# Identity matmuls of TensorE in the opening and the tail, stores moved to POOL, and a planner with other constants

## The chip, the cores and the metric

One core of a Trainium2 chip runs the whole program. The metric is the device time of one execution in microseconds (us). TensorE (PE) multiplies, with weight loads on a track of their own (PEld); VectorE (DVE) and ScalarE (ACT) do elementwise work and empty the accumulator banks; GpSimd (POOL) and SyncE (SP) mostly issue DMAs.

## What is computed

```python
B, S, D = 8, 3136, 256                     # d_qk = 64
scores = (1.0 / S) * np.matmul(z, z.transpose(0, 2, 1))
attn = np.maximum(scores, 0.0) ** 2
x = u * np.matmul(attn, v)

proj = x @ w_proj                          # D -> 3 D
x1, x2, x3 = proj[..., :D], proj[..., D:2 * D], proj[..., 2 * D:]
X2 = np.fft.rfft(x2, n=S, axis=1)
H = np.fft.rfft(filter_fft, n=S, axis=0)[None]
x2_conv = np.fft.irfft(X2 * H, n=S, axis=1)
out = (x1 * x2_conv * x3) @ w_out
```

Inputs and output are float32; the kernel multiplies in bfloat16 and accumulates in float32.

## The kernel before

The sequence of 3136 is written as 64 x 49, so that the Fourier transform splits into a stage over 64 and a stage over 49, both done as matmuls. The sequence is cut into 25 tiles of 128 rows (the last has 64) and, for the query side, into seven chunks of 512, 512, 512, 512, 512, 256 and 320 columns. The work of one batch is:

- Scores, kind "S": zT against itself, 64 rows deep, two or four matmuls side by side in the array, into a pair of banks (`ps_s`). ACT applies the relu (`R_t`, line 1767), DVE or ACT squares (`A_t`, lines 1776 and 1774).
- Weighing, kind "W": v against the squares, accumulated in two banks of their own (`ps_o`). Some squares are used a second time as their mirror images: SP transposes them by DMA into `M_t`, `M2e_t`, `M2o_t` (line 1700). DVE multiplies the sum by u (`xT_t`, line 1818).
- Projection, kind "FA" (for the last batch partly "FZ"): to the gates (`to_gates`: x1 and x3, copied as `x_t` and multiplied on DVE into `gate_t`, line 1160), and to the spectrum (`to_spectrum`: x2, then the first stage of the transform, stored to a scratch in DRAM by line 964).
- Spectrum, kind "Q" (`add_spectrum`): loads of the scratch (line 994), the second stage as quads of 64 x 64 tiles, two multiplications by H on DVE (line 1248), inverse quads, copies into `gs_t` (for the last batch also `M2o_t`, `A_t`, `uT_t`), and stores to a second scratch (`put`, line 1293).
- End, kinds "FB" and "FZ" (`add_end`): loads of the second scratch (line 1006), the last stage of the inverse with T, the product with the gates on DVE (`yT_t`, line 1334), the product with w_out, the copy to `ost_t` (or another free tile) and the store to the output (`store`, line 1394).

No engine's order is written out by hand. The kernel makes tasks with costs, and a planner (`Plan.go`) lays them out: again and again it takes, over all five queues, the task that can start first by its own clock, emits it, and notes when its results and buffers will be there. For PE it chooses among the kinds (`pick_pe`), by the fields of `RULES`: whether weighing work left over (`backlog`, `ample`) is enough to wait for banks, how long it stays with the scores while the next pair is not free (`stay`), when quads go ahead (`first`, `lead`), and when projections and ends may go before weighing (`pace`, `full`). For work that either DVE or ACT can do, `pick` decides, with `give` as the weight of the tasks that would be held up on the second engine. It charges PE 0.096 us whenever it goes between the scores' tile shape and full-array work. A change of a constant, of a cost or of a due time (`late`) therefore can change the order on every engine.

Banks: three pairs for scores and quads; single banks of the same pairs for projections and ends (`one_slots`).

The ends of a batch are interleaved with the next batch's attention. For the last batch but one (b = 6) three chunks are ended so and four are held back, kind "FZ", until the last batch needs something to do while its spectrum goes through DRAM. For the last batch (b = 7) the chunks end in the order `FINAL`, and its outputs go in two halves, one from POOL and one from SP; the last chunk goes from SP alone:

```python
            if split and c == cs[-1]:
                for k, e_ in enumerate(oe):
                    s_ = on("SP", lambda i0=2 * k, n=min(2, nt - 2 * k), store=store: store(i0, n), 0.9, [e_, *behind], prio=1, moves=0.9)
```

The opening: SP loads z of the first batch in three parts, POOL loads v and u with a cast, POOL and DVE make the identity (`ident`) that PE's transposes need, and the DFT tables are made on DVE, ACT and PE beside the first attention.

Of the kernel before, what the change touches and what calls it, by code (L numbers as in the profile page):

```python
# [12 lines left out]
P = 128  # L13
# [15 lines left out]
SPEC_LAG = 1  # L29
LATE_F = 6.0  # L30
LATE_OUT = 2.0
AFTER = (1, 3, 5, 6)
FINAL = (0, 2, 4, 6, 1, 3, 5)
ZP, ZL = 0, 0.0
# [1 line left out]
REACH = 2  # L36
Rule = namedtuple("Rule", "backlog ample stay first lead pace full give")
STEP = 50.0
RULES = [Rule(0.5, 5.0, 0.15, 0, 1, 0.55, 3.5, 0)]
SHARE = {0: 1, 2: 3}  # L40

ISSUED = "issued"
# [14 lines left out]
def c_pe(*ns):  # L57
    return sum(n / 2400 + 0.003 for n in ns)
# [123 lines left out]
class Plan:  # L182
# [151 lines left out]
    def pick(self, e):  # L334
# [18 lines left out]
                best = (key, s, task)  # L353
        return best and (best[1], best[2], e)

    def go(self):
        while True:
            got = []
            x = self.pick_pe()
            if x:  # L360
                got.append((x[0], 0, x[1], "PE", x[2]))
            for i, e in enumerate(self.pend):
                x = self.pick(e)
                if x:
                    got.append((x[0], i + 1, x[1], e, None))
            if not got:
                break
            start, _, task, e, k = min(got, key=lambda g: g[:2])
            if k:
                self.queues[k].remove(task)  # L370
                half = k in ("S", "Q")
                if half != (self.mode == "S") and self.mode:
                    start += 0.096
                    self.quarters, self.quad_run, self.score_run = half and self.soon, 0, 0
                self.score_run += k == "S"
                if k == "Q":
                    self.quad_run += 1
                    if self.score_run and not self.quarters:
                        start += 0.092
                    self.quarters = True  # L380
                self.mode = "S" if half else k
                if k == "W":
                    self.credit = min(self.credit + self.rule(start).pace, 2.0)
                elif k != "S":
                    self.credit = max(self.credit - task.cost["PE"], -2.0)
            self.run(task, e, start)
        left = sum(len(q) for q in self.queues.values()) + sum(len(q) for q in self.pend.values())
        assert not left, f"{left} tasks left over"
# [3 lines left out]
def kernel(  # L392
# [307 lines left out]
    plan.free["POOL"] = 12.0  # L700
    plan.free["SP"] = 3.0
    plan.free["DVE"] = 1.5


    def after(task, at):
# [282 lines left out]
    def load_spec(src, j0, nj, deps, late=0.0, home=l_p):  # L988
        box = {}

        def go():
            box["t"] = home.tile([P, 8, D], BF16)
            for rows, part in by_row(src, box["t"], 2 * j0, 2 * nj):
                nc.sync.dma_start(out=part, in_=rows)

        t = on("SP", go, 1.3, [*deps, *((d, ISSUED) for d in loads[-1:])], [home.slots], moves=0.6 * nj, late=late)
        return in_order(t), box

    def load_c(src, c, deps, home):
        t0, nt = T0[c], len(tiles[c])  # L1000
        box = {}

        def go():
            box["t"] = home.tile([P, 4, D], BF16)
            view = src[ds(t0 * P, nt * P), :].rearrange("(t p) d -> p t d", t=nt)
            nc.sync.dma_start(out=box["t"][:, 0:nt, :], in_=view)

        if home is c_p:
            return in_order(on("SP", go, 0.45, [*deps, *((d, ISSUED) for d in loads[-1:])], [home.slots], moves=0.4 * nt, late=LATE_C)), box
        return on("SP", go, 0.45, deps, [home.slots], moves=0.4 * nt), box  # L1010

    def sides(x):
        return x[:, 0:D], x[:, D : 2 * D]
# [200 lines left out]
    def add_spectrum(b, puts):  # L1214
# [9 lines left out]
        for g in range(NJ // 2):  # L1224
            own = not final or g % 2 == 0
            xh = xh_p if own else R_p
            mine = set_of[g]
            per, gh = 2 * len(mine), outs[sets.index(mine)]
            if g % 2 == 0:
                ldb[0] = load_spec(D1[b % 2], 2 * g, 4, puts, LATE_LOAD * (not final), homes[g // 2] if final else l_p)  # L1230
            ld, ibox = ldb[0]
            xb = {}

            def mm(ps, g=g, xb=xb, ibox=ibox, xh=xh):
                xb["x"] = xh.tile([P, 2, 4, D], BF16)
                forward(ps, slot(ibox["t"], 2 * g % 4), g)

            def ev(e, h, p, xb=xb):
                copy(e, xb["x"][:, 0, ds(2 * h, 2), :].rearrange("p c d -> p (c d)"), p)

            a0, evs = add_quads(mm, ev, c_quads(g), [ld, *deps0], [xh.slots])
            if g % 2:
                a0.frees.append((ld, 0))

            def mul(i, g=g, xb=xb):
                x = xb["x"][:].rearrange("p i (j c) d -> p i j c d", c=2)
                h = H[:, ds(2 * g, 2), i].unsqueeze(2).to_broadcast([P, 2, 2, D])
                nc.vector.tensor_tensor(x[:, 1 - i], x[:, 0], h, ALU.mult)  # L1248

            def add(xb=xb):  # L1250
                x = xb["x"][:].rearrange("p i (j c) d -> p i c j d", c=2)
                nc.vector.tensor_tensor(x[:, 1, 0], x[:, 1, 0], x[:, 0, 1], ALU.subtract)
                nc.vector.tensor_tensor(x[:, 1, 1], x[:, 1, 1], x[:, 0, 0], ALU.add)

            cost = c_dve2(4 * D)
            w_ = on("DVE", lambda mul=mul: mul(0), cost, evs, prio=ZP)
            w_ = on("DVE", lambda mul=mul: mul(1), cost, [w_], prio=ZP, lat=ZL)
            z_ = w_ if final else on("DVE", add, 2 * c_dve2(2 * D), [w_], prio=ZP)

            def inv(g=g, xb=xb, z_=z_, a0=a0, gh=gh, mine=mine, per=per):  # L1260
                new = g == mine[0]
                if new:
                    gb[0] = {"es": [], "firsts": []}
                gx = gb[0]

                def mm(ps, g=g, new=new):
                    if new:
                        gx["g"] = gh.tile([P, 2 * per, D], BF16)
                    z, y = (slot(xb["x"][:, i], 0) for i in range(2))
                    if final:  # L1270
                        inverse2(ps, y, z, g)
                    else:
                        inverse(ps, y, g)

                def ev(e, h, p, g=g):
                    copy(e, gx["g"][:, ds(2 * (2 * (g - mine[0]) + h), 2), :].rearrange("p c d -> p (c d)"), p)

                a, evs = add_quads(
                    mm, ev, c_quads(g, 1 + final), [z_, *gx["firsts"], *(minus_task if final else [])], [gh.slots] if new else []
                )  # L1280
                gx["firsts"] = [a]
                if new:
                    gx["g0"] = a
                a.frees.append((a0, 1))
                inverses.append(a)
                gx["es"] += evs
                if g != mine[-1]:
                    return
                j0 = 2 * mine[0]

                def put():
                    for rows, part in by_row(D2[b % 2], gx["g"], 2 * j0, 2 * per):
                        nc.sync.dma_start(out=rows, in_=part)

                p_ = on("SP", put, 1.2, gx["es"], moves=0.5 * per, late=LATE_D2 * (not final))
                p_.frees.append((gx["g0"], 1))
                lasts.append(p_)

            behind.append(inv)
            if g >= SPEC_LAG:  # L1300
                behind.pop(0)()
# [4 lines left out]
    def add_end(b, lasts, gtasks, cs, kind="FB", src=c_p, dsts=(o_p,), late=0, behind=(), then=(), split=False, mids=(y_p,)):  # L1306
        for at, c in enumerate(cs):
            t0, nt = T0[c], len(tiles[c])
            w = CHUNKS[c]
            dst, mid = dsts[at % len(dsts)], mids[at % len(mids)]  # L1310
            ld, cb = load_c(D2[b % 2], c, lasts, src)
            yb = {}
            ys = []
            firsts = []
# [33 lines left out]
                ys.append(e_)  # L1348
            ob = {}
            oe = []  # L1350
            for i0 in range(0, nt, 2):
                n = min(2, nt - i0)
                last = min(P, w - (i0 + n - 1) * P)
                box = {}

# [38 lines left out]
                        by.dma_start(out=r[:, n2 : n2 + hi - lo, :], in_=ob["o"][ds(j * N1, N1), i0 : i0 + hi - lo, :])  # L1394

            if split and c == cs[-1]:
                for k, e_ in enumerate(oe):
                    s_ = on("SP", lambda i0=2 * k, n=min(2, nt - 2 * k), store=store: store(i0, n), 0.9, [e_, *behind], prio=1, moves=0.9)
            elif split:
                s_ = on("POOL", lambda nt=nt, store=store: store(0, nt, (0,), nc.gpsimd), 0.6, [*oe, *behind], moves=0.22 * nt)  # L1400
                s_ = on("SP", lambda nt=nt, store=store: store(0, nt, (1,)), 0.8, [*oe, *behind], prio=1, moves=0.22 * nt)
            else:
                s_ = on("SP", lambda nt=nt, store=store: store(0, nt), 1.3, [*oe, *behind], prio=1, moves=0.45 * nt, late=LATE_OUT * (dst is o_p))
# [508 lines left out]
```

## Time and profile before

| | us |
|---|---|
| three runs, median (lowest to highest) | 992.51 (992.26 to 992.87) |
| the profiled execution | 993.72 |
| its span, first to last instruction | 991.5 |

Busy time over the span:

| engine | busy us | share | instructions |
|---|---|---|---|
| PE | 958.2 | 97% | 6831 |
| PEld | 472.2 | 48% | 6831 |
| ACT | 867.9 | 88% | 1187 |
| DVE | 819.4 | 83% | 1465 |
| POOL | 191.7 | 19% | 409 |

The chain of work that ended last is 82% PE, 7% DVE, 4% ACT and 2% DMA. Matmuls are pipelined and their ends are modelled, so a busy PE is not a PE at its peak: the distance between two starts says how fast it streams. POOL issues DMAs of the software kind, which took 2.5 to 5.3 us from issue to landing, by size. On the last row of POOL stands a drain of 8.45 us, from 982.3 us on.

By stage, idle time of PE (length less busy time): 7.9 us from 0 to 10, 1.5 us from 10 to 20, 0.6 us from 20 to 30, 1.5 us from 30 to 40, 4.6 us in the 800 us from 100 to 900, 4.0 us from 940 to 960, 1.7 us from 960 to 970, 1.3 us from 970 to 980. After 981.8 us no matmul runs.

### The profile page before, as it was taken

What the parts mean: (1) busy time and instruction counts of PE and PEld (TensorE: products, weight loads), DVE (VectorE), ACT (ScalarE), POOL (GpSimd) and SP (SyncE); (2) the same over time, 40 slices, a digit from 0 to 9 for tenths busy, and PEclk for the clock granted to TensorE, in tenths of its full rate; (3) what the DMA queues carried; (4) which work ended last, traced back from release to release, by engine and by line L of the source; (5) the groups of instructions that cost most, each with busy time, mean ns of one, the idle gap of its engine ahead of it and who ended that gap; (6) DMA issues with size and microseconds to landing.
All of it is one profiled execution on the core that took longest, in us unless ns stands there. A gap on an engine that the chain in (4) does not pass through costs nothing.

```text
span 991.5 us, 19534 instructions
## 1 busy us (share of the span) xinstructions
PE 958.2 (97%) x6831; PEld 472.2 (48%) x6831; DVE 819.4 (83%) x1465; ACT 867.9 (88%) x1187; POOL 191.7 (19%) x409
## 2 busy tenths in 40 slices
PE   6999999999999999999999999999999999999985
PEld 2344544455444554446444454444544455544643
DVE  7876689987899878987789877898779988799774
ACT  6988898988998898899989999889989899999773
POOL 5132311132013210313111220121202231001001
PEclk9999999999999999999999999999999999999978
DMA  9889958979979799978998786998889978984576
GB/s 154 150 171 199 165 118 128 187 137 185 202 174 176 147 194 187 186 156 133 200 197 178 148 152 152 205 191 158 153 196 186 203 138 165 202 213 106 154 229 197
DMA packets 332343, 170.32 MB, mean 172 GB/s; under 512 B 242442, under 2 KB 307786, under 8 KB 332244
## 3 DMA queue, kind: packets, MB, share of 16 engines
q1 hardware_dynamic: 304068, 136.59, 63.4%
q0 software_dynamic: 28176, 32.48, 23.2%
q8 instruction: 54, 0.88, 0.4%
q14 instruction: 45, 0.37, 0.1%
HBM read 90.26 MB, written 53.35 MB: 145 GB/s over the span
## 4 chain that ended last, share of the span: by engine, by line
PE 82%; DVE 7%; ACT 4%; DMA 2%; issue 2%; SPq 1%; POOL 0%; POOLq 0%; DVEq 0%; ACTq 0%
PE ps_o_t L521 48%; PE ps_s L521 34%; DVE A_t L1776 2%; ACT R_t L1767 2%; DVE xT_t L1818 1%; DMA M2e_t<-A_t 1%; DVE xh L1248 1%; DMA ost_t<-in_z_dram 1%; DMA conv_in_t<-spec 1%; DVE gate_t L1160 1%; DVE yT_t L1334 1%; SPq L646 1%; ACT A_t L1774 0%; ACT x_t L554 0%; DMA M_t<-A_t 0%
## 5 line engine op out<-in xcount | busy, mean ns | idle before, releaser
L1767 ACT ACTIVATE R_t<-ps_s 128x1024 f32<-128x1024 f32 (+4 forms) x512 | 466.9, 963 | 57.1 <-PE ps_s L521 55.0
L521 PE MATMUL ps_o_t<-A_t,v_t 128*128 128x512 bf16 (+3 forms) x2084 | 459.5, 354 | 2.9 <-DVE A_t L1776 2.1
L521 PEld LDWEIGHTS <-v_t 128*128 128x128 bf16 (+2 forms) x2878 | 250.6, 98 | 257.8 <-issue 73.2
L1776 DVE TENSOR_TENSOR A_t<-R_t 128x1024 bf16<-128x1024 f32 (+3 forms) x283 | 313.9, 1123 | 64.2 <-ACT R_t L1767 61.1
L1774 ACT ACTIVATE A_t<-R_t 128x1024 bf16<-128x1024 f32 (+3 forms) x213 | 211.7, 1007 | 3.1 <-DMA M2e_t<-A_t 1.7
L521 PE MATMUL ps_s<-zT_t 64*64 64x512 bf16 (+5 forms) x1485 | 170.8, 361 | 2.0 <-ACT R_t L1767 1.0
L604 POOL COPY tick<-xT_t 1x1 bf16<-1x1 bf16 x54 | 13.8, 256 | 681.6 <-DVE xT_t L1818 681.6
L521 PEld LDWEIGHTS <-zT_t 64*64 64x64 bf16 (+1 forms) x1518 | 53.9, 101 | 109.7 <-issue 93.7
L521 PE MATMUL ps_s<-xT_t,wp 128*128 128x512 bf16 (+2 forms) x430 | 103.7, 353 | 2.4 <-DVE gate_t L1160 0.9
L554 ACT ACTIVATE x_t<-ps_s 128x512 bf16<-128x512 f32 (+2 forms) x148 | 81.7, 583 | 19.7 <-PE ps_s L521 12.5
L1818 DVE SCALAR_TENSOR_TENSOR xT_t<-ps_o_t,uT_t 128x256 bf16<-128x256 f32 (+2 forms) x224 | 76.1, 381 | 22.8 <-PE ps_o_t L521 14.4
L1248 DVE TENSOR_TENSOR xh<-xh,H 128x1024 bf16<-128x1024 bf16 x120 | 82.0, 683 | 2.1 <-ACT xh L554 0.9
L521 PE MATMUL ps_o_t<-M_t,v_t 128*128 128x512 bf16 (+2 forms) x352 | 81.8, 353 | 0.0
L1160 DVE TENSOR_TENSOR gate_t<-ps_s,x_t 128x256 bf16<-128x256 f32 (+2 forms) x216 | 71.2, 381 | 6.6 <-PE ps_s L521 4.6
L1334 DVE TENSOR_TENSOR yT_t<-ps_s,gate_t 128x512 bf16<-128x512 f32 (+2 forms) x99 | 57.9, 613 | 10.3 <-PE ps_s L521 10.0
L558 DVE CAST xh<-ps_s 128x512 bf16<-128x512 f32 x71 | 47.3, 685 | 22.8 <-PE ps_s L521 19.5
L521 PEld LDWEIGHTS <-wp 128*128 128x128 bf16 x448 | 42.3, 98 | 49.6 <-issue 15.2
L595 POOL DMA_DIRECT2D un_t<-in_u_dram x112 | 59.8, 554 | 5.6 <-issue 2.7
L614 POOL DMA_DIRECT2D v_t<-in_v_dram x112 | 59.4, 552 | 6.4 <-issue 3.8
L521 PE MATMUL ps_s<-wp,xT_t 128*128 128x256 bf16 x398 | 56.7, 272 | 0.5 <-ACT R_t L1767 0.3
L521 PE MATMUL ps_s<-wo,yT_t 128*128 128x256 bf16 (+1 forms) x344 | 52.0, 273 | 1.6 <-DVE yT_t L1334 1.3
L554 ACT ACTIVATE s_t<-ps_s 128x512 bf16<-128x512 f32 (+1 forms) x79 | 44.9, 592 | 5.5 <-PE ps_s L521 2.1
(154 smaller groups left out, 833.1 us busy)
## 6 DMA issues: line engine op xcount, KB each, us to landing
out_dram<-ost_t SPq DMA_DIRECT2D x66, 256.0 KB
spec<-s_t SPq DMA_DIRECT2D x96, 128.0 KB
spec_in_t<-spec SPq DMA_DIRECT2D x60, 192.0 KB
spec<-gs_t SPq DMA_DIRECT2D x60, 192.0 KB
v_t<-in_v_dram POOLq DMA_DIRECT2D x80, 128.0 KB, 4.5
un_t<-in_u_dram POOLq DMA_DIRECT2D x80, 128.0 KB, 4.9
conv_in_t<-spec SPq DMA_DIRECT2D x33, 256.0 KB
out_dram<-ost_t SPq DMA_DIRECT2D x19, 128.0 KB
```

What stands on the lines that cost most here:

```text
L521: wrote(nc.tensor.matmul(o, *args, **kw), o)
L554: got = nc.scalar.activation(out_, in_, AF.Copy)
L558: got = nc.vector.tensor_copy(out_, in_)
L595: nc.gpsimd.dma_start(out=t[ds(j * N1, N1), lo - t0 : hi - t0, :], in_=x[:, n2 : n2 + hi - lo, :])
L614: nc.gpsimd.dma_start(out=t[ds(j * N1, N1), ds(v_at(a), (b - a) * D)], in_=r[:, n2 + a - lo : n2 + b - lo, :].rearrange("p t d -> p (t d)"),)
L1160: got = nc.vector.tensor_tensor(g[:, ::-1] if h == 0 else g, p, x, ALU.mult)
L1248: nc.vector.tensor_tensor(x[:, 1 - i], x[:, 0], h, ALU.mult)
L1334: got = nc.vector.tensor_tensor(yb["y"][:, dh, 0:w], p, gates[b, c, dh][:, 0:w], ALU.mult)
L1767: has_read(nc.scalar.activation(blocks(box["R"], n, cw)[:rows], p, AF.Relu), p)
L1774: nc.scalar.activation(a, r, AF.Square)
L1776: nc.vector.tensor_tensor(a, r, r, ALU.mult)
L1818: nc.vector.scalar_tensor_tensor(x, f, inv_s2, ut, ALU.mult, ALU.mult)
```

## The change

- Fillers. Before the planner emits a task, `fill` looks whether PE is free long enough before it. In the opening (before 13 us of the plan's time), or when no scores and no weighing are left, it emits a matmul of the identity by the identity, 128 x 512, into a free single bank, as long as it ends 0.25 us before the next task is due. Its result is not read. In the opening a filler is charged double. PE counts as free from 1.8 us on.
- Outputs of b = 6 are stored from POOL instead of SP.
- Spectrum of the last batch: of the three stores of each set, SP issues one or two (two for the last two sets) and POOL the others.
- Last chunk of the last batch: its two tiles are multiplied and copied one by one, and its two halves are stored from SP and from ACT.
- The rule has other constants, and the loads of the spectrum and of some chunks other costs for the planner.

```diff
+LATE_POOL = 1.2
+WARM, SPARE = 13.0, 0.25
-RULES = [Rule(0.5, 5.0, 0.15, 0, 1, 0.55, 3.5, 0)]
+RULES = [Rule(1.25, 5.0, 0.05, 0.5, 1, 0.5, 3.0, 1.0)]
...
+    def fill(self, until):
+        t = self.free["PE"]
+        opening = t < WARM
+        cost = c_pe(512) * (1 + opening)
+        if not opening and (self.queues["S"] or self.queues["W"] or not any(self.queues.values())):
+            return False
+        start = t + 0.096 * (self.mode == "S")
+        if until < start + cost + 0.096 * (self.mode == "S") + SPARE or self.singles.when() > start:
+            return False
+        self.bank, self.got = self.singles, [(self.singles, self.singles.take(start))]
+        self.filler()
+        self.free["PE"] = start + cost
+        self.singles[self.got[0][1]] = start + cost
+        if self.mode:
+            self.mode, self.quarters = "W", False
+        return True
...
             start, _, task, e, k = min(got, key=lambda g: g[:2])
+            if self.fill(start):
+                continue
...
+    plan.free["PE"] = 1.8
+    plan.singles = one_slots
+    plan.filler = lambda: matmul(bank(), ident[:], ident[:].unsqueeze(1).to_broadcast([P, 4, P]), start=True, stop=True)
...
-        t = on("SP", go, 1.3, [*deps, *((d, ISSUED) for d in loads[-1:])], [home.slots], moves=0.6 * nj, late=late)
+        t = on("SP", go, 1.6, [*deps, *((d, ISSUED) for d in loads[-1:])], [home.slots], moves=0.4 * nj, late=late)
...
-        return on("SP", go, 0.45, deps, [home.slots], moves=0.4 * nt), box
+        return on("SP", go, 0.55, deps, [home.slots], moves=0.3 * nt), box
...
-                def put():
-                    for rows, part in by_row(D2[b % 2], gx["g"], 2 * j0, 2 * per):
-                        nc.sync.dma_start(out=rows, in_=part)
-
-                p_ = on("SP", put, 1.2, gx["es"], moves=0.5 * per, late=LATE_D2 * (not final))
+                def put(part=slice(0, 3), by=nc.sync):
+                    for rows, t in by_row(D2[b % 2], gx["g"], 2 * j0, 2 * per)[part]:
+                        by.dma_start(out=rows, in_=t)
+
+                if final:
+                    n = 1 + mine[0] // 2 % 2
+                    p_ = on("SP", lambda: put(slice(0, n)), 0.55 * n, gx["es"], moves=0.25 * per)
+                    lasts.append(
+                        on("POOL", lambda: put(slice(n, 3), nc.gpsimd), 0.55 * (3 - n), gx["es"], moves=0.25 * per, late=LATE_POOL)
+                    )
+                else:
+                    p_ = on("SP", put, 1.2, gx["es"], moves=0.5 * per, late=LATE_D2)
...
+            step = 1 if split and c == cs[-1] else 2
...
-            for i0 in range(0, nt, 2):
-                n = min(2, nt - i0)
+            for i0 in range(0, nt, step):
+                n = min(step, nt - i0)
...
             if split and c == cs[-1]:
-                for k, e_ in enumerate(oe):
-                    s_ = on("SP", lambda i0=2 * k, n=min(2, nt - 2 * k), store=store: store(i0, n), 0.9, [e_, *behind], prio=1, moves=0.9)
+
+                def both_queues(nt=nt, store=store):
+                    store(0, nt, (0,))
+                    store(0, nt, (1,), nc.scalar)
+
+                s_ = on("SP", both_queues, 0.6, [*oe, *behind], prio=1, moves=0.45 * nt)
+            elif b == B - 2:
+                s_ = on(
+                    "POOL", lambda nt=nt, store=store: store(0, nt, by=nc.gpsimd), 1.2, [*oe, *behind],
+                    moves=0.45 * nt, late=LATE_POOL,
+                )
```

## The prediction

> **What bounds the kernel now.** I read the slices of busy time first, then the busy time by stage.
>
> ```profile
> PE   6999999999999999999999999999999999999985
> PEclk9999999999999999999999999999999999999978
> ...
> 0.00:10.00 10.00, 2.12 (x10) 0.76 (x11) 6.73 (x37) 4.88 (x8) 8.32 (x25) 1.00 0.79 147
> 10.00:20.00 10.00, 8.49 (x52) 3.96 (x51) 7.43 (x16) 6.60 (x9) 5.14 (x11) 1.00 1.03 173
> 20.00:30.00 10.00, 9.38 (x50) 3.27 (x49) 9.99 (x10) 7.66 (x8) 0.00 (x0) 1.00 1.22 145
> ...
> 700.00:800.00 100.00, 99.98 (x689) 47.38 (x691) 84.64 (x146) 89.44 (x117) 16.80 (x34) 1.00 0.94 183
> ...
> 940.00:960.00 20.00, 16.05 (x191) 10.32 (x192) 16.75 (x29) 15.55 (x31) 0.00 (x0) 0.78 0.87 247
> 960.00:970.00 10.00, 8.26 (x55) 4.19 (x55) 6.00 (x15) 4.73 (x10) 0.00 (x0) 0.75 0.49 147
> 970.00:980.00 10.00, 8.69 (x95) 6.82 (x94) 8.33 (x18) 5.27 (x11) 2.16 (x4) 1.00 0.79 225
> ```
>
> The columns of a stretch are its length, busy time of PE, PEld, DVE, ACT and POOL, granted clock, DMA share and GB/s. PE is the bound from about 40 to 940 us: the eight stretches of 100 us from 100 to 900 leave 4.6 us of PE idle in all. Only the opening and the tail have room, and only the tail shows a clock below 1. Cut finer, the clock is 1.00 up to 951.3, 0.50 from 951.4 to 965.0 and 1.00 again until 985. In the opening that column has no record before about 12 us, so there I read spacing in the order of time:
>
> ```profile
> 11.40 2.10 PE L521 MATMUL ps_o_t<-A_t,v_t 128*128 128x512 bf16 x6
> ...
> 12.90 1.04 ACT L554 ACTIVATE xT_t<-ost_t 128x448 bf16<-128x448 f32 x2 [2.49 <-DMA ost_t<-in_z_dram]
> ...
> 16.20 1.02 PE L521 MATMUL ps_o_t<-A_t,v_t 128*128 128x512 bf16 x4 [0.30 <-DVE A_t L1776]
> ```
>
> The first six matmuls of 512 columns start 0.42 us apart up to 12.68 us and 0.22 us apart after it, as the four at 16.20 do: PE runs at half speed until about 12.7 us. But what is waited for at 12.9 us is the third load of z.
>
> Last the tail, where I followed the queues beside PE:
>
> ```profile
> 936.59 4.04 SPq L1394 DMA_DIRECT2D out_dram<-ost_t  x4
> 940.72 3.52 SPq L994 DMA_DIRECT2D spec_in_t<-spec  x6
> ...
> 962.43 2.01 SPq L1293 DMA_DIRECT2D spec<-A_t  x3
> 964.54 1.32 SPq L1293 DMA_DIRECT2D spec<-uT_t  x3
> 967.09 4.09 SPq L1006 DMA_DIRECT2D A_t<-spec  x7
> ...
> 962.39 1.89 PE L521 MATMUL ps_o_t<-xT_t,wp 128*128 128x512 bf16 x4
> 964.07 1.49 PE L521 MATMUL ps_s<-xT_t,wp 128*128 128x512 bf16 x4
> ```
>
> The last batch's spectrum loads stand behind four output stores of the batch before; its last spectrum stores stand in one queue, and the loads of its inverse wait for them. The eight gate matmuls at 962.39 take 3.4 us for what eight times 0.216 us would be.
>
> **The change part by part.**
>
> *Fillers.* The built program's order has 38 of them on PE: 12 before and between the first z transposes and scores, 26 from the last batch's spectrum on. At 0.43 us cold the opening's cost 5.2 us, at 0.216 us the tail's cost 5.6 us; both lie in time in which the plan has PE waiting. If the cover is gone, a filler delays what stands behind it by its own length, and in the tail by two changes of tile shape more (about 0.10 us each, below).
>
> Opening: seven fillers begin when the identity is there (1.6 us), so the clock is up somewhere between 5 and 9 us instead of 12.7. What then runs at full speed is the second z transpose (1.06 us), six weighings (2.10 us) and the second scores: about 1.4 us earlier at 13.4 us. The third z load at 12.9 does not move, and the order now gives its two casts that ACT did (0.57 us each) to DVE, ahead of a square of 1.22 us, so most is lost again, and from 20 to 30 us DVE is busy 9.99 of 10. Bounds: 2.2 us gained (half of the 4.4 us that matmuls stream at half speed before 12.7, summed from their starts), 0.9 lost (two late fillers). I take **-0.7**, nearer the third load.
>
> Tail, multiplications by H (947 to 961): DVE works through 16 of 0.60 us and eight copies almost without gaps, and one copy of 0.6 us goes to ACT; a clock at full speed shortens the last quads and the first waits (0.44, 0.38 and 0.16 us on DVE). **-0.9**, bounds -1.5 and 0.
>
> Tail, gates (962 to 970.7): eight matmuls at full clock save 3.4 - 1.7 = 1.7 us, if the loads behind come as early. SP begins the stores of uT_t at 964.54 although the copies ended at 963.2, because A_t's three were still being issued; now SP issues two of each three and POOL the third (0.55 us, in parallel). The last SP issue ends about 1.7 us earlier, but POOL's small DMAs (8 KB of z) landed 2.5 us after issue, so I count 0.9 for the queue and 0.5 for the copies: loads from 965.7, not 967.09. **-1.4**, bounds -1.9 and 0.
>
> *Stores of batch 6 on POOL.* Fourteen issues of 0.54 us, 7.6 us, on a queue that was idle from 916 to 975; behind them now stand POOL's seven spectrum stores, not due before 953. SP's loads at 940.72 can go once the stores of s_t have landed, 2.6 to 3.2 us earlier. But the order also moves 3.3 to 3.5 us of end work of batch 6 and gates (16 matmuls with wo among it) to before the last weighing: from 931.3 to the first spectrum matmul PE had 12.9 us of stream in 15.7 us; now it has 9.6 us in 12.5 us. The wait stays 2.8 us and the gain is used up: **0**, bounds -1.6 (all of the idle) and +1.2 (the landing later than I think).
>
> *Last chunk.* One copy of 0.60 us becomes two of 0.38 us, and its second store goes from SP to ACT. But the last engine to finish is POOL: its last store is issued at 982.33 and its closing drain lasts 8.45 us, while SP has finished at 988.1 and waits until 990.9. The chunk's stores are off that path: 0 from this, **-0.3** for the work in front of it, bounds -0.8 and +0.3.
>
> *New constants of the rule and new costs.* They reorder the 900 us in between. The count of runs of scores and quads that interrupt full-array matmuls goes from 289 to 297; by the starts in the trace the median change of shape costs 0.096 us in and 0.105 to 0.125 us out, so +1.7. Against it 23 squares of 1024 move from ACT to DVE and copies move back: at the means by shape (1.218 us on DVE, 1.078 us on ACT; copies 0.685 and 0.61) DVE gets 8.7 us busier and ACT 9.8 us less busy, of 819 and 868. ACT carries the relus that free the banks for the scores. Bounds: -2.9 (all 4.6 us of idle gone, less 1.7) and +10.4 (all of DVE's 8.7 seen by PE, plus 1.7). I take **0**: the runs' price is paid back by ACT's relief.
>
> Sum: -0.7 - 0.9 - 1.4 + 0 - 0.3 + 0 = **-3.3 us**. The profiled execution took 993.72 us, 2.2 us of it outside the span of 991.5; it becomes 990.4. The median of the runs is 1.2 us below that execution, so I forecast 992.5 - 3.3 = **989.2 us**.
>
> [...]
>
> **The rivals.**
>
> *The clock falls anyway.* From 951.4 to 961.5 PE was called busy 8.5 of 10.1 us, but by quads of a quarter of the array, and the clock came back only after 3.3 us of full-array gates. The fillers are full-array, but between the first spectrum matmul and the gates there are 18, 3.9 us in some 15. If that is too thin, the multiplications keep 0.5 of 0.9 at most and the gates 0.9: -0.7 - 0.5 - 0.9 + 0.3 = -1.8, **990.7 us**. Against it: the clock held until 951.3 through 937 to 947, where PE was far from full.
>
> *ACT was the hidden wait.* If its relief ends all PE idle in the middle (-2.9) and the tail reaches its bounds (another -1.2), **985.1 us**. For it: ACT is at 90% there and the waits for a free bank end on relus; against it, the rows leave only 4.6 us.
>
> *DVE becomes what the weighings wait for.* Place: 50 to 930 us, the matmuls into ps_o_t. A square on DVE takes 0.14 us longer, and DVE gets 8.7 us more work. If half of that shows on PE (4.4) and nothing is paid back for the runs (1.7), the middle costs 6.1: **995.3 us**. It decides once about 3.6 of the 8.7 us surface. Against it: PE waited for squares only 2.1 us in all; for it: PE has no slack of its own, so whatever is late there stays.
>
> **How the numbers follow.** Forecast 0.45, clock 0.16, ACT 0.15, DVE 0.24. Differences within 0.2%, about 2 us, can't be told from none. The forecast and ACT's case are faster: 0.60. The clock's is the same: 0.16. DVE's is slower: 0.24. The range goes from just below ACT's case to DVE's, 984.5 to 995.5; the forecast's own is 987 to 991.
>
> **What would show it.** Matmuls of 512 columns 0.22 us apart from 9 us on, not 13; a granted clock of 1.00 from 940 to 980; SP's loads of spec_in_t directly behind the stores of s_t; spec<-uT_t within 0.3 us of its copies; first matmul T,A_t about 2 us earlier after the last weighing; PE idle of about 4.6 us in the middle stretches. The forecast is wrong if the middle shifts by more than 2 us, which the last weighing's place shows (931 us before, 3.5 us of moved work on top), or if POOL's drain grows with its 21 more stores.

## The result, and the profile after

| | before | after |
|---|---|---|
| runs on the same chip, median (lowest to highest), us | 992.38 (992.05 to 992.87) | 998.47 (996.59 to 999.5) |
| the profiled execution, us | 993.72 | 999.5 |
| its span | 991.5 | 997.7 |

The ratio is 1.0055, 95% interval 1.0042 to 1.0068: slower by 5.5 us, where 3.3 us faster was forecast. The interval is from four runs; the kernel with the same program except for six stores (e12 below) spread from 988.8 to 1000.2 us in eleven runs, so the size is known less well than the interval says.

First the slices of the page, then the stretches, of the changed kernel (columns as before: length, busy time of PE, PEld, DVE, ACT, POOL, granted clock, DMA share, GB/s):

```profile
PE   7998999999999999999999999999989999999985
PEclk9999999999999999999999999999999999999998
```

```profile
0.00:10.00 10.00, 6.18 (x26) 2.01 (x27) 7.35 (x39) 5.29 (x8) 8.47 (x25) 1.00 0.76 146
...
90.00:95.00 5.00, 4.95 (x27) 2.39 (x27) 3.89 (x6) 2.55 (x4) 0.29 (x1) 1.00 1.26 149
95.00:100.00 5.00, 2.30 (x16) 1.03 (x14) 1.01 (x2) 3.78 (x6) 0.00 (x0) 1.00 1.11 153
...
700.00:800.00 100.00, 95.13 (x654) 44.63 (x663) 84.00 (x146) 87.51 (x116) 18.10 (x39) 0.98 0.92 177
...
940.00:960.00 20.00, 16.96 (x169) 10.42 (x167) 15.30 (x32) 13.06 (x27) 6.05 (x12) 1.00 0.72 228
960.00:970.00 10.00, 8.48 (x119) 3.88 (x121) 7.95 (x14) 7.39 (x15) 3.17 (x6) 1.00 0.47 124
```

The fillers do what the change says: the tail, which was at 0.78 and 0.75, is at 1.00 throughout, and the clock is up at 4.4 us. What is new stands in the middle, where PE had almost no idle time before. From 95 to 100 us it is busy 2.30 of 5 us, and from 700 to 800 us it loses 4.9 us and a little of its clock.

The waits of PE from 50 to 930 us (us in all, times, longest) say for what. Changed kernel, then the kernel before:

```profile
PE ps_o_t L542 <- issue: 4.3, 27, 0.2
PE ps_o_t L542 <- DVE xT_t L1859: 2.6, 5, 1.1
PE ps_s L542 <- ACT s_t L575: 2.6, 1, 2.6
PE ps_s L542 <- DMA spec_in_t<-spec: 2.5, 2, 1.9
PE ps_s L542 <- DVE xT_t L1859: 1.5, 7, 0.3
```

```profile
PE ps_o_t L521 <- DVE xT_t L1818: 0.5, 1, 0.5
PE ps_s L521 <- DVE xT_t L1818: 0.4, 2, 0.2
```

The first row is no wait: this trace has 6784 matmuls for 6881 weight loads, and the 27 gaps are places where a matmul's record is missing. The trace of e12 (below), with the same order and 6881 of both, has no such row. Two single waits, of 2.6 us at 95 us and of 1.9 us (with 0.6 behind it) at 738 us, are the largest; the second is followed by a clock of 0.50 from 741.7 to 745.1. The waits for `xT_t`, which DVE makes from the sums of the weighings, grew from 0.9 to 4.1 us.

To place the loss I take the time at which the last weighing is read (the last `xT_t` on DVE):

| us, profiled executions | before | after | difference |
|---|---|---|---|
| last weighing read | 932.0 | 942.1 | +10.1 |
| from there to POOL's closing drain | 50.3 | 44.4 | -5.9 |
| the drain | 8.45 | 10.27 | +1.8 |
| from there to the end of the span | 0.8 | 0.9 | +0.1 |

Of the 10.1 us, 3.5 are matmuls that the new order streams ahead of the last weighing instead of behind it (36 of them, with 8192 columns in all, counted in e12's trace, at 0.216 us for 512 columns, the distance of two starts at full clock in both traces), so the middle lost 6.6 us net and the tail's work gained 2.4. Of the 6.6, 2.0 are 20 more changes of tile shape at 0.1 us; the opening stood 1.6 us earlier, though the trace of before is the latest of ten there (34.1 us where their mean is 33.0); waits and the half clock make up the rest, some 6.2. This sum closes only to a few us: by their rows, the waits from 50 to 930 us grew by 8.0 (from 3.6 to 11.6 us, missing records left out).

### The profile page after: what moved, and what is told of

It is laid out like the page before. It is cut to its first block, busy times and chain, and to the rows that moved or that the text cites. A ratio compares the mean times of both kernels' runs of the same rounds, so it can differ in the third digit from the quotient of the medians.

```text
span 997.7 us, 19593 instructions
## 1 busy us (share of the span) xinstructions
PE 951.8 (95%) x6784; PEld 471.1 (47%) x6881; DVE 831.6 (83%) x1463; ACT 861.3 (86%) x1190; POOL 205.8 (21%) x430
## 5 line engine op out<-in xcount | busy, mean ns | idle before, releaser
L542 PE MATMUL ps_o_t<-A_t,v_t 128*128 128x512 bf16 (+3 forms) x1992 | 446.2, 353 | 11.0 <-issue 4.4
L1817 DVE TENSOR_TENSOR A_t<-R_t 128x1024 bf16<-128x1024 f32 (+3 forms) x306 | 343.3, 1133 | 62.4 <-ACT R_t L1808 61.7
L542 PEld LDWEIGHTS <-v_t 128*128 128x128 bf16 (+1 forms) x2878 | 251.0, 98 | 259.2 <-issue 67.9
L1815 ACT ACTIVATE A_t<-R_t 128x1024 bf16<-128x1024 f32 (+3 forms) x190 | 186.0, 990 | 5.2 <-issue 3.7
L542 PE MATMUL ps_s<-zT_t 64*64 64x512 bf16 (+4 forms) x1497 | 173.9, 366 | 3.7 <-ACT s_t L575 2.6
L625 POOL COPY tick<-xT_t 1x1 bf16<-1x1 bf16 x54 | 16.9, 313 | 703.2 <-DVE xT_t L1859 703.2
L575 ACT ACTIVATE x_t<-ps_s 128x512 bf16<-128x512 f32 (+2 forms) x155 | 85.5, 586 | 23.0 <-PE ps_s L542 17.5
L1184 DVE TENSOR_TENSOR gate_t<-ps_s,x_t 128x256 bf16<-128x256 f32 (+2 forms) x216 | 71.8, 384 | 11.9 <-PE ps_s L542 10.1
L575 ACT ACTIVATE s_t<-ps_s 128x512 bf16<-128x512 f32 (+1 forms) x92 | 53.6, 602 | 7.2 <-PE ps_s L542 6.6
L542 PE MATMUL ps_s<-wo,yT_t 128*128 128x256 bf16 (+1 forms) x364 | 55.3, 275 | 0.8 <-DVE yT_t L1366 0.6
```

Source lines behind the costliest of these rows:

```text
L542: wrote(nc.tensor.matmul(o, *args, **kw), o)
L575: got = nc.scalar.activation(out_, in_, AF.Copy)
L1184: got = nc.vector.tensor_tensor(g[:, ::-1] if h == 0 else g, p, x, ALU.mult)
L1815: nc.scalar.activation(a, r, AF.Square)
L1817: nc.vector.tensor_tensor(a, r, r, ALU.mult)
```

## The experiments

All runs of one session share the kernel before as their yardstick. "Order kept" means that PE, DVE and ACT execute the same instructions in the same order as in the kernel before, fillers apart.

| run | kernel | median us (lowest to highest) | before | ratio, 95% |
|---|---|---|---|---|
| e1 | before, order kept, all fillers | 994.69 (993.92 to 996.78) | 992.52 | 1.0028 (1.0016 to 1.0040) |
| e2 | before, new constants of the rule | 992.68 (991.31 to 994.46) | 992.52 | 1.0004 (0.9995 to 1.0013) |
| e3 | before, both new load costs | 996.69 (995.47 to 998.7) | 992.52 | 1.0049 (1.0034 to 1.0064) |
| e4 | after, old constants | 999.91 (998.08 to 1001.53) | 992.52 | 1.0077 (1.0058 to 1.0095) |
| e5 | after, old load costs | 996.90 (995.07 to 998.07) | 992.77 | 1.0038 (1.0026 to 1.0051) |
| e6 | after, no fillers | 995.89 (992.15 to 999.67) | 992.77 | 1.0031 (1.0015 to 1.0047) |
| e7 | before, order kept, stores as changed | 993.03 (991.46 to 995.63) | 992.77 | 1.0003 (0.9990 to 1.0015) |
| e8 | e7 with all fillers | 995.77 (994.37 to 997.86) | 992.77 | 1.0029 (1.0017 to 1.0041) |
| e9 | before, order kept, POOL's last six stores on SP | 990.44 (989.55 to 991.92) | 992.25 | 0.9979 (0.9970 to 0.9988) |
| e10 | before, order kept, 16 fillers of the tail | 990.47 (989.23 to 991.6) | 992.25 | 0.9980 (0.9969 to 0.9991) |
| e11 | before, order kept, 11 fillers of the opening | 993.26 (991.14 to 995.91) | 992.25 | 1.0010 (0.9999 to 1.0021) |
| e12 | after, POOL's last six stores on SP | 994.83 (988.8 to 1000.24) | 992.25 | 1.0018 (0.9997 to 1.0038) |
| e13 | before, new cost of a spectrum's load | 996.55 (995.1 to 997.8) | 992.46 | 1.0041 (1.0028 to 1.0053) |
| e14 | before, new cost of a chunk's load | 990.43 (989.21 to 992.11) | 992.46 | 0.9977 (0.9968 to 0.9986) |
| e15 | after, old constants up to 150 us | 991.49 (990.43 to 994.68) | 992.46 | 0.9991 (0.9981 to 1.0002) |
| e16 | the order before, the useful parts in the tail | 988.76 (986.67 to 990.18) | 992.46 | 0.9957 (0.9941 to 0.9972) |
| e17 | e15, POOL's last six stores on SP | 989.01 (987.44 to 992.86) | 992.87 | 0.9962 (0.9948 to 0.9976) |
| e18 | after, four loads of v later | 993.53 (992.16 to 1002.7) | 992.87 | 1.0027 (1.0006 to 1.0048) |

### One part at a time: e1 to e4

```diff
# e1: the planner's order is left alone; a filler is emitted into a free bank before a task that starts late
+            self.fill(start)
# e2
+RULES = [Rule(1.25, 5.0, 0.05, 0.5, 1, 0.5, 3.0, 1.0)]
# e3
+        t = on("SP", go, 1.6, [...], [home.slots], moves=0.4 * nj, late=late)
+        return on("SP", go, 0.55, deps, [home.slots], moves=0.3 * nt), box
# e4: the changed kernel with
+RULES = [Rule(0.5, 5.0, 0.15, 0, 1, 0.55, 3.5, 0)]
```

e1: 

> The kernel before with fillers alone (11 in the opening, 36 in the tail), put into an order that is otherwise the same, instruction for instruction, on every engine. Plan theory (the middle of 900 us was laid out worse, fillers and moved stores are a small gain): 989.5 to 991.5 us, chunk (0,2) about 2 us earlier than in the kernel before, the clock at full speed to the end. Filler theory (the fillers hold up what stands behind them): 994 us or more.

e2: 

> The kernel before with the new constants of the rule alone. If the rule lays the middle out worse: 996 to 1001 us, with the attention of the last chunk (7,6) ending 5 to 9 us later. If the loss is from the new costs of the loads or from the fillers: 990.5 to 994 us.

e3: 

> The kernel before with the new costs of the two loads alone. If these make the plan start quads before their load has landed (as at 737 us of the changed kernel): 995 to 999 us, with single waits of PE of 1 to 3 us on loads of spec_in_t. If the rule is the cause: 990.5 to 994 us.

e4: 

> The changed kernel with the old constants of the rule; fillers, moved stores and new costs stay. If the rule is the cause: 988 to 991 us. If the costs of the loads are: 996 us or more. If any new layout of the middle is worse than the one of before, whichever constant changed: 993 to 999 us.

The new constants alone change nothing (e2), and taking them out of the changed kernel doesn't help (e4). The load costs alone cost 4.2 us, and the fillers alone 2.2 us, though they hold the clock in the tail. e1 came out as its filler theory says, e2 in the range for another cause, e3 in its first range and e4 in that of the load costs. The parts don't add up, because constants and costs each make the planner lay out another order. A price of one part can be read from the runs with the order kept, or between two kernels that share an order.

Up to the last weighing the traces show only a few orders. PE, DVE and ACT execute the same instructions in the same order, fillers apart, in the changed kernel, e6, e12 and e18; in e2 and e5; in e3 and e4; and in e15 and e17.

### Fillers and stores with the order kept: e5 to e8, e10, e11

```diff
# e5, e6: the changed kernel with the old load costs; without
-            if self.fill(start):
-                continue
# e7, e8: the kernel before, and e1, with the changed store queues
+                        (nc.sync if i < n else nc.gpsimd).dma_start(out=rows, in_=part)
+                        store(i0, n, (0,))
+                        store(i0, n, (1,), nc.scalar)
+                ... store(0, nt, by=nc.gpsimd if b == B - 2 else nc.sync)
# e10 and e11: e1 with only these fillers (n = whether in the opening, and its number)
+            if not n[0] and n[1] < 16:
+            if n[0]:
```

e5: 

> The changed kernel with the two load costs as before (1.3 and 0.6 for a spectrum's load, 0.45 and 0.4 for a chunk's); all else as changed. Theory A, the new load costs plan the loads of spec_in_t and of the chunks so that PE waits on them: the 4 us that the costs alone added go away, 993.5 to 995.5 us, and the last weighing comes 4 us earlier than in the changed kernel. Theory B, the fillers and the rest of the order cost it and the load costs only matter in the order of before: it stays at 997.5 to 999.5 us.

e6: 

> The changed kernel without any filler matmul; all else as changed, the planner's order free to move. Theory A, the load costs set the time and fillers add about 2 us as they did by themselves: 996 to 997.5 us. Theory B, fillers and the order that they push the planner into are the larger part: 992 to 994.5 us. If the fillers are worth what the prediction says once the stores are split (opening 0.7, multiplications 0.9, gates 0.9), the time without them is longer, 1000 to 1001.5 us.

e7: 

> The kernel before with its order kept instruction for instruction on PE, DVE and ACT; only the issuing queue of some stores changes: batch 6's output stores on POOL, each third part of the last spectrum's stores on POOL, half of the last chunk's stores on ACT. The prediction's terms for these without a warm clock: stores of batch 6 up to 1.2 us gained since no end work is moved here, gates 0.5 to 0.9, last chunk 0: 990.8 to 992.0 us. Rival, POOL's stores land later than SP's and its closing drain grows with 21 more stores: 993 to 995 us.

e8: 

> As the run with the stores alone, plus the 47 fillers of the run with the fillers alone, order of all else as before. If the fillers cost 2.2 us wherever they stand, this is the time of the stores alone plus 2.2 us (993 to 994.2 us). If the loads behind the stores were what kept the fillers' full clock in the tail from showing, it is 989.5 to 991.5 us, below both.

e10: 

> The kernel before, its order kept, with only the first 16 of the tail's fillers (from the last batch's spectrum to the gates); none in the opening, and not the 20 that stand before and among the first inverse multiplications. Theory A, those 20 delay the inverse by 2.7 us, as the gap between their start and the loads' landing says, and the clock that the 16 hold is worth the 1.7 us that the eight gate matmuls save, less some 0.5: 990.8 to 991.7 us. Theory B, the end of the gates doesn't set the rest: 992.2 to 992.8 us.

e11: 

> The kernel before, its order kept, with only the 11 fillers of the opening. Theory A, the opening gains about 0.9 us at the first weighings and keeps it: 991.5 us. Theory B, the early clock moves the casts, copies and stores of the first chunks against each other, and a wait later in the first batch takes it back or more (in the run with all fillers the gain of 0.93 was gone at 87 us and a loss of 0.8 stood at 127 us): 992.5 to 993.5 us.

e5 and e6 fell between their theories: 1.6 us and 2.6 us less than the changed kernel, with e6 spread over 7.5 us. e7 came out as its rival says, 0.3 us over the kernel before. e8 came out above both of its theories, 2.7 us over e7, and its order of time shows why. First e8:

```profile
965.20 3.73 SPq L1031 DMA_DIRECT2D A_t<-spec  x7
...
968.55 3.62 PE L544 MATMUL ps_s<-ident 128*128 128x512 bf16 x16
972.00 0.61 PE L544 MATMUL ps_s<-T,A_t 128*128 128x128 bf16 x8
```

Then e10, whose fillers end before the gates do:

```profile
966.15 3.71 SPq L1035 DMA_DIRECT2D A_t<-spec  x7
...
967.83 0.43 PE L548 MATMUL ps_s<-xT_t,wp 128*128 128x320 bf16 x2
969.07 0.62 PE L548 MATMUL ps_s<-T,A_t 128*128 128x128 bf16 x8 [0.81 <-DMA A_t<-spec]
```

And the kernel before:

```profile
970.45 0.43 PE L521 MATMUL ps_s<-xT_t,wp 128*128 128x320 bf16 x2
970.72 0.39 PE L521 MATMUL ps_s<-T,A_t 128*128 128x128 bf16 x4
```

In e10 the first inverse matmul runs 2.9 us after the first load of A_t is issued. In e8 the loads go 0.95 us earlier, so by the same 2.9 us the data would be there at about 968.1 (an estimate), but 16 fillers stand in the queue until 972.0: the planner believed the loads later than they are, and filled. T,A_t starts only behind the last of them. The gates end at 968.5, so some 3.4 us are lost there; with the block left out the held clock is worth 1.8 us (e10, a little better than expected). The lines also show that before the change the loads were not waited for at all: T,A_t follows the gate matmuls directly. Only when the clock shortens the gates do the loads become what is waited for (0.81 us).

The opening's fillers gain nothing. The first chunk's weighings are read at 33.02 us on average in the ten executions without them (32.5 to 34.1) and at 32.98 us in the ten with them (32.1 to 34.0). e11 gives +1.0 us with an interval that touches zero, inside its theory B. In e11's own trace the 11 fillers don't raise the clock before 13.0 us (12.7 in the kernel before). In the other nine traces with them it is up between 4.4 and 9.1 us, but in seven of the nine it falls to half once more for 3.4 or 6.8 us before 23 us; in the changed kernel and e18 it does not.

### The end of the program: e9, e12

```diff
# both: in the line of the "split" outputs
-                s_ = on("POOL", lambda nt=nt, store=store: store(0, nt, (0,), nc.gpsimd), ...
+                s_ = on("POOL", lambda nt=nt, store=store: store(0, nt, (0,), nc.sync), ...
```

e9: 

> The kernel before, its order kept, with the last six output stores that POOL issued (975.2 to 982.9 us) issued by SP instead, so that POOL's last transfer is some 60 us before the end. Theory A, POOL's closing drain (8.45 us from its last store, the last thing to end) sets the end: the drain lies early and the program ends by SP, which was done at 988.1 us and has six more issues of 0.5 us, of which one or two are in the way: 989.5 to 990.7 us. Theory B, the drain only waits for the last transfer to land, whoever issued it: 992 us or more.

e12: 

> The changed kernel with the last six output stores of POOL issued by SP. If POOL's closing drain, which takes 9.6 to 10.3 us in the five kernels with the 21 added POOL stores and 8.1 to 8.9 us in the four without, is what ends the changed kernel: 994.5 to 996 us, by SP's last stores. If the drain is a shadow of the last landing: 998 us or more.

Both came out as the first theory says, e12 with executions spread over 11.4 us. In e9 the drain runs from 913.5 to 921.0 us and nothing waits for it. The trace has a drain in every run:

| DMAs that POOL issued in the run | the closing drain, us |
|---|---|
| 325 (e9) | 7.49 |
| 331 (eight runs, the kernel before among them) | 8.04 to 8.89, mean 8.44 |
| 346 (e12, e16, e17) | 9.13, 9.16, 9.13 |
| 352 (eight runs, the changed kernel among them) | 9.60 to 10.34, mean 10.01 |

The 21 stores that the change gives to POOL lengthen the drain by 1.6 us (8.44 to 10.01; 7.49 to 9.14), 0.08 us each. The six output stores just before it lengthen it by 0.9 us in both pairs, 0.15 us each. So the number is not all that counts. All these stores lie in the program's last 80 us, so whether earlier DMAs lengthen it isn't shown. In e7 the stores on other queues gained nothing ahead of it (50.6 us from the last weighing to the drain, 50.3 before), and the drain was 1.2 us longer.

### The load costs: e13, e14

```diff
# e13
+        t = on("SP", go, 1.6, [...], [home.slots], moves=0.4 * nj, late=late)
# e14
+        return on("SP", go, 0.55, deps, [home.slots], moves=0.3 * nt), box
```

e13: 

> The kernel before with the cost of a spectrum's load alone as changed (1.6 and 0.4 instead of 1.3 and 0.6). Theory A, this reorders the middle so that PE waits on spec_in_t and the 4 us of both costs are all here: 996 to 998 us. Theory B, the chunk's load does it: 992 to 993 us.

e14: 

> The kernel before with the cost of a chunk's load alone as changed (0.55 and 0.3 instead of 0.45 and 0.4), which leaves the order untouched up to the last batch. Theory A, the shorter tail of the run with both costs comes from here: 989.5 to 991.5 us. Theory B, the tail's length hangs on the middle's order, not on this: 992 to 993 us.

They pull in opposite directions: the spectrum's load costs 4.1 us, by way of the whole middle; the chunk's load, which changes nothing before the last batch, gains 2.0, and its tail from the last weighing to the drain is 47.6 us where it was 50.3. Both fell in the range of their theory A. But e3, with both, costs 4.2 us, as much as e13: in that order the chunk's gain doesn't show. Through which waits e13 loses I can't say: its trace has no wait on spec_in_t as long as in e3 (1.6 us), and no single wait above 1.1 us. The theory was right on the place and not shown on the mechanism.

### The wait at 95 us: e15, e18

```diff
# e15: the changed kernel with
+RULES = [Rule(0.5, 5.0, 0.15, 0, 1, 0.55, 3.5, 0)] * 3 + [Rule(1.25, 5.0, 0.05, 0.5, 1, 0.5, 3.0, 1.0)]
# e18: the changed kernel with
-                        load_rows(v16[n], v[n], lo, hi)
+                        if (n, c) != (1, 3):
+                            load_rows(v16[n], v[n], 8 if (n, c) == (1, 4) else lo, hi)
```

e15: 

> The changed kernel with the rule's old constants up to 150 us and the new ones after. Theory A, the new constants cost through the squares that wait on ACT for a buffer between 82 and 105 us (1.6 to 3.2 us of PE, and a half clock for 3.4 us in some runs): the stall there goes and the time is 995 to 997 us. Theory B, they cost through the later order or not at all, and the load costs decide: 998 to 1000 us.

e18: 

> The changed kernel with the four loads of the next batch's v that POOL issues at 87.1 us moved behind its step at 105 us; every order but POOL's as changed. Theory A, they fill the transfer engines, so that the transposing transfer issued at 88.87 us lands only at 96.2 us and the square that waits for its buffer holds up ACT and PE: the wait of 2.8 us at 95 us goes, 994.5 to 996.5 us. Theory B, the transfer is late for another reason (the stores and transposes in SP's own queue): the wait stays, 997.5 to 999.5 us.

e15 was 7.0 us below the changed kernel (6.4 by the ratios), better than either theory; but its order differs to the end (16 changes of shape fewer up to the last weighing), so it isn't the price of the first 150 us alone. e18 changes POOL's queue and nothing else. The order of time of the changed kernel:

```profile
87.14 2.11 POOL L635 DMA_DIRECT2D v_t<-in_v_dram  x4
88.87 3.83 SPq L1741 DMA_TRANSPOSE M2e_t<-A_t  x2
...
96.22 1.06 ACT L1815 ACTIVATE A_t<-R_t 128x1024 bf16<-128x1024 f32 x1 [3.68 <-issue]
97.19 0.58 ACT L575 ACTIVATE s_t<-ps_s 128x512 bf16<-128x512 f32 x1
...
97.82 0.77 PE L542 MATMUL ps_s<-zT_t 64*128 64x256 bf16 x6 [2.61 <-ACT s_t L575]
...
729.93 2.80 SPq L1426 DMA_DIRECT2D out_dram<-ost_t  x4
732.77 3.62 SPq L1018 DMA_DIRECT2D spec_in_t<-spec  x6
...
739.77 0.40 PE L542 MATMUL ps_s<-spec_in_t,S 49*64 49x256 bf16 x2 [1.91 <-DMA spec_in_t<-spec]
```

and of e18, its stretch from 90 to 95 us first:

```profile
90.00:95.00 5.00, 5.00 (x27) 2.34 (x27) 3.89 (x6) 4.56 (x7) 0.00 (x0) 1.00 0.32 75
```

```profile
88.97 3.83 SPq L1742 DMA_TRANSPOSE M2e_t<-A_t  x2
...
92.50 1.08 ACT L1816 ACTIVATE A_t<-R_t 128x1024 bf16<-128x1024 f32 x1
...
94.92 0.71 PE L542 MATMUL ps_s<-zT_t 64*128 64x256 bf16 x9
```

Read the first from below. PE waits for a bank that ACT's copy `s_t` empties; the copy stands behind a square on ACT that starts 3.68 us late. The profile gives no releaser for it, but the trace's wait in front of it is on the signal of the transposing transfer issued at 88.87, which reads the square's buffer. It lands at 96.2, 7.3 us after its issue, while the DMA share is 1.26. In e18, with the next batch's v out of the way, the share is 0.32, the same transfer is done before the square asks (92.50, no wait), and the scores run through at 94.92. Theory A holds for the wait; the median came out 1.0 us below its range. The kernel is 4.9 us faster by the medians and 2.8 us by the ratios (1.0027 against 1.0055, with intervals that still touch); its single executions still reach 1002.7 us, so it has other costs that come in some executions only.

The order alone doesn't make the wait, though. e6 has the changed kernel's order there on every engine, fillers apart, and its loads of v are not moved:

```profile
89.80 2.11 POOL L633 DMA_DIRECT2D v_t<-in_v_dram  x4
...
93.12 3.84 SPq L1739 DMA_TRANSPOSE M2e_t<-A_t  x2
...
98.04 1.06 ACT L1813 ACTIVATE A_t<-R_t 128x1024 bf16<-128x1024 f32 x1 [1.24 <-issue]
```

Here the transposing transfer is issued 3.3 us after the loads of v, not 1.7, and its signal is there 4.9 us later; ACT waits 1.24 us and PE 0.2. In e12 it is issued 1.7 us after them, its signal takes 7.7 us, and PE waits 3.0. e2, with another order, has a like wait of 1.4 us of PE after 95 us and is no slower than the kernel before. So the loads of v delayed the transfer when they went just ahead of it (7.3 and 7.7 us to its signal with 1.7 us between them, 4.9 us with 3.3), but what this one wait costs the whole program is not shown. In the one order of the changed kernel, e6, e12 and e18 the last weighing is read at 942.1, 938.6, 942.4 and 934.8 us.

The wait at 738 us looks alike: loads of spec_in_t issued behind four output stores of 256 KB, landing 7.0 us after the first issue. No run tested that one, but it belongs to this execution and not to the order: from 50 to 930 us e12 and e18 show no wait for spec_in_t, and e6 one of 0.5 us.

### What the parts make together: e16, e17

```diff
# e16: the kernel before with e14's cost, the changed store queues, e9's line, and of the fillers only
+            if not n[0] and n[1] not in range(9, 99):
# e17: e15 and e9's line
```

e16: 

> The middle of the kernel before; in the last batch the chunk's new load cost, nine fillers from the spectrum to the gates and none before the inverse, the stores split over the queues as changed, but POOL's last six output stores on SP. By the sum of the runs so far (drain 1.8 gained, held clock 1.8 gained, the order of the last batch 0 to 1): 987.5 to 989.5 us. If the gains of the clock and of the drain are the same microseconds, because SP's own end then sets the time: 990 to 991 us.

e17: 

> The changed kernel with the old constants up to 150 us (as in the run before, 991.5 us) and POOL's last six output stores on SP. There POOL's drain ended the program at 988.2 us of the span, while SP's last store was issued by 980.2 us: if the drain alone sets the end, 987 to 988.5 us; if the stores moved to SP make SP late by as much, 990 us or more.

Both beat both kernels, by 3.7 and 3.9 us against the kernel before, and can't be told apart. e16 came out inside its first range. e17 gained 2.5 us over e15 and fell between its theories: SP's last store, with six more in the queue, was issued 4 us later after the last weighing than in e15, so part of the drain's time came back.

## Why the prediction was wrong

- **What failed:** the step "New constants of the rule and new costs", taken at 0. In the profiled execution the middle lost some 8.2 us (6.6 and the opening's 1.6). By themselves the load costs cost 4.2 us (e3) and the constants nothing (e2). The bounds held it; the value did not. Its pieces: the price of the shape changes was right (1.7 predicted, 2.0 counted). ACT's relief did not pay it back. What wasn't in the sum at all is that instructions in a new place meet transfers: a square on ACT was to fill a buffer that a transposing DMA still read, at a place where the DMA share was 1.26, and everything behind it in ACT's queue waited. That is one wait of 2.6 us, shown by e18; the others, and those through which the load costs act, are not traced to a cause. I had seen a DMA share of about 1 in the early stretches and drew nothing from it.
- **The other parts did not gain their 3.3 us either.** By the ratios, fillers and stores cost 2.9 us in the order of before (e8), and fillers, stores and last chunk cost 3.4 us with the new constants (e5 against e2) and 2.8 us with the new load costs (e4 against e3). These kernels have 16, 18 and 7 fillers in front of the inverse and the changed kernel four, so the price need not be the same there, and no run has constants and costs together without the rest. How the 5.5 us divide between middle and tail is therefore read from one trace of each kernel.
- **One step lumped what should have been split.** Each alone, the two load costs have opposite signs, +4.1 and -2.0 us, and the second acts on the tail alone, where I could have costed it.
- **Multiplications and gates (-0.9 and -1.4):** the clock's part was about right. e10 gives -1.8 us with nothing but the clock, and T,A_t 1.5 us earlier after the last weighing. Wrong was that the loads set the start of the inverse before the change; they were off the path (T,A_t follows the gate matmuls at 970.72). So the split stores alone gained nothing (e7); that they gain once the clock is held is argued, not shown by a run of its own. The cover I named for the fillers, time in which the plan has PE waiting, held for 16 of e1's 36 and failed for the block before the inverse. In the changed kernel that block has four fillers, with the old load costs 18 (e5): the new costs make the planner expect the loads earlier.
- **Opening (-0.7):** nothing, 33.0 us with and without. That the clock would be up between 5 and 9 us was my estimate: it was up at 4.4 us in the changed kernel, but only at 13.0 us in e11.
- **Stores of batch 6 and last chunk (0 and -0.3):** I read that POOL's drain ends the program, and costed 21 more stores in that queue at nothing. They cost 1.6 us. It was named as what would make the forecast wrong, without a price.
- **Rivals.** "The clock falls anyway" is refuted: 1.00 to the end of the tail in the changed kernel, e1, e8 and e10. With nine fillers (e16) it held through the gates and fell for 3.4 us at 970.3. "ACT was the hidden wait" fails, since ACT with less work held PE up more. "DVE becomes what the weighings wait for" gave the nearest time, 995.3 us, and named the right stretch; PE's waits on DVE's xT_t did grow, from 0.9 to 4.1 us, but the two largest waits end on ACT's queue and on DMAs, of which it said nothing. That its time came near is in part luck.

## What to carry over

When an edit changes a planner's constants, price the new order by its new neighbours, not by the engines' totals: look for instructions that wait for a buffer which a DMA still reads, and at what stands behind them in their queue, above all where the DMA share is high (1.26 at the wait here, 0.32 in the run without it). To price one part of such a change, keep the order and change that part alone, or compare two kernels whose traces show the same order; and take several executions, since one order's last weighing came at 934.8 to 942.4 us here. A filler is free only if the wait it fills is real, and a queue whose closing drain ends the program should stop issuing early: six stores on another queue were worth 1.8 us here.

## Of the hardware, not expected

- POOL's closing drain was longer the more DMAs POOL had issued: 7.49 us for 325, 8.44 us on average for 331, 9.13 to 9.16 us for 346, and 10.01 us on average for 352.
- A transposing DMA took 7.3 us from issue to its signal behind POOL's loads (DMA share 1.26), 7.7 us in e12, 4.9 us in e6, where the loads went further ahead, and at most 3.5 us in e18 without them (issued at 88.97 us, no wait of the square at 92.50; share 0.32).
- In the changed kernel waits of PE of 1.9 and 0.6 us were followed by a half clock for 3.41 us (741.7 to 745.1 us); one of 2.6 us at 95 us was not, while a like wait was in e5 (98.1 to 101.5 us) and e12 (100.9 to 104.3 us). e12 has the changed kernel's order there, so the order doesn't decide it; that it is a part of why the executions of one kernel differ is a guess. The half-clock stretches up to the end of the tail lasted 3.41 us in the changed kernel and 13.65 us in the kernel before (951.4 to 965.0 us, where PE was busy 3.23 of the first 3.50 us).
